# Linear attention on one core: the first head's k and v move from SyncE's DMA queue to ScalarE's

## The chip, the core and the metric

The kernel runs on one NeuronCore of one Trainium2 chip. A core has five engines with an instruction stream each: TensorE (PE, matrix products and transposes), VectorE (DVE), ScalarE (ACT), GpSimd (POOL) and SyncE (SP), which here only issues transfers. Transfers between HBM and the on-chip memory are carried out by 16 DMA engines, which are fed through queues; an engine that issues a transfer puts it into its own queue and goes on. The metric is the time of one execution on the device in microseconds; of several executions the median counts.

## The reference

For each of 32 heads (sequence length S = 2048, head width D = 128, bf16), linear attention with the feature map elu(x) + 1:

```python
phi_q = jnp.where(q > 0, q + 1, jnp.exp(q)) + 1e-6
phi_k = jnp.where(k > 0, k + 1, jnp.exp(k)) + 1e-6
kv = jnp.einsum("bhsd,bhse->bhde", phi_k, v)
z = jnp.einsum("bhsd->bhd", phi_k)
num = jnp.einsum("bhqd,bhde->bhqe", phi_q, kv)
den = jnp.einsum("bhqd,bhd->bhq", phi_q, z)[..., None] + 1e-6
return num / den
```

q, k and v have the shape (1, 32, 2048, 128), and so has the result. A head of one of these tensors is 512 KB.

## The kernel before

**Tiling.** A head is laid out as 128 partitions by 16 tiles of 128 elements, so that a load or store of a head moves 128 rows of 4096 bytes. The feature map is computed as min(exp(x), 1) + 1e-6 plus max(x, 0), and the two summands are kept apart: every product is two accumulating matmuls.

**Stages of a head h.** Each operation has a key, a letter code with the head and a part number:

- `ldk`, `ldq`, `ldv` (line 324) load k, q and v of the head into one of NI = 7 buffers each.
- For k: `ek` (line 336, ACT) takes the exponential, `em` (line 339, DVE) the minimum with 1 and the addition; `rkd` (line 342, DVE) and `rkp` (line 346, POOL) take max(k, 0) of one half each.
- `v1` (line 350, POOL) copies v beside a column of ones; `kv` (line 357, PE) makes the 128 x 129 matrix of kv and z, and `kvs` (line 362, ACT) copies it out.
- For q: `T` (line 368, PE) transposes q; `eq` (line 372, ACT), `emq` (line 374, DVE), `rqa` (line 378, ACT) and `rqb` (line 381, DVE) apply the feature map.
- `n` (lines 389, 394, 396, PE) makes numerator and denominator; `r` (line 403, DVE) is the reciprocal of the denominator and `f` (line 410, DVE) the product with it; `st` (line 418) stores the head.

In head 0 the operations on k, q and v are cut into two halves (parts .0 and .1), but its three loads are whole heads. The last head is cut more finely, its store into three parts.

**Order.** What each engine does in which order is written out by hand in the table `ORDER` (line 83). A small planner, `Program.resolve` (line 182), turns the dependencies between keys into semaphore waits; an engine works through its list strictly in order. PE begins with two groups of dummy matmuls on the identity matrix, `w2` and `w1` (4 each, line 315), then the two halves of `T0`, then `w0` (15 dummy matmuls), then `kv0`. ACT begins with

```python
eq0.0 eq0.1 ek0.0 ek0.1 rqa0 ek1.0 kvs0 eq1.0 rqa1 ek2.0 kvs1 ...
```

and SP, which issues every load and every store, begins with

```python
ldq0.0 ldk0.0 ldv0.0 ldk1.0 ldq1.0 ldv1.0 ldk2.0 ldq2.0 ldk3.0 ldv2.0 ldv3.0 ...
```

The first 21 loads have no buffer to wait for; a later one waits until its buffer has been read. Every load slot has a semaphore of its own; each of the 16 DMA engines raises it by one when its share has landed, and the reader waits for all 16. SP ends by waiting for all stores.

**Buffers that tie engines together.** `em`, `rk`, `v1`, `emq`, `rq` and `kvs` have two buffers each, so an engine may be at most two heads ahead of its reader. Through a `gate`, POOL starts `rkp` and `v1` of head h only after `f` or `r` of head h - 3.

Of the kernel before, what the change touches and what calls it, by code (L numbers as in the profile page):

```python
# [4 lines left out]
ACT = mybir.ActivationFunctionType  # L5
# [5 lines left out]
NI, NO, NE, NR, NV, NQ, NK = 7, 12, 2, 2, 2, 2, 2  # L11
WARM = (15, 4, 4)
HALVES = ((0, 8), (8, 16))
WHOLE = ((0, 16),)


def k_parts(h):
    return HALVES if h == 0 else WHOLE


def ld_parts(h):
    return WHOLE

# [4 lines left out]
def q_parts(h):  # L28
    return HALVES if h == 0 else ((0, 8), (8, 12), (12, 16)) if h == NH - 1 else WHOLE


def kv_parts(h):
    return HALVES

# [23 lines left out]
def st_parts(h):  # L58
    return ((0, 6), (6, 12), (12, 16)) if h == NH - 1 else WHOLE

# [10 lines left out]
def t_parts(h):  # L71
    return HALVES if h in (0, NH - 1) else WHOLE


def rqb_parts(h):
    if na(h) == 16:
        return ()
    if h == NH - 1:
# [34 lines left out]
        emq31.1 f29.1 r30.0 f30.0 r30.1 f30.1 r31.0 f31.0 r31.1 r31.2 f31.1 f31.2  # L113
    """,
    "ACT": """
        eq0.0 eq0.1 ek0.0 ek0.1 rqa0 ek1.0 kvs0 eq1.0 rqa1 ek2.0 kvs1 ek3.0 eq2.0 rqa2 kvs2 ek4.0 eq3.0 kvs3 rqa3
        ek5.0 eq4.0 kvs4 rqa4 ek6.0 eq5.0 kvs5 rqa5 ek7.0 eq6.0 kvs6 rqa6 ek8.0 eq7.0 kvs7 rqa7 ek9.0 eq8.0 kvs8
        rqa8 ek10.0 eq9.0 kvs9 rqa9 ek11.0 eq10.0 kvs10 rqa10 ek12.0 eq11.0 kvs11 rqa11 ek13.0 eq12.0 kvs12 rqa12
        ek14.0 eq13.0 kvs13 rqa13 ek15.0 eq14.0 kvs14 rqa14 ek16.0 eq15.0 kvs15 rqa15 ek17.0 eq16.0 kvs16 rqa16
# [10 lines left out]
        v128.0 rkp28.0 v129.0 rkp29.0 v130.0 rkp30.0 v131.0 rkp31.0  # L130
    """,
    "SP": """
        ldq0.0 ldk0.0 ldv0.0 ldk1.0 ldq1.0 ldv1.0 ldk2.0 ldq2.0 ldk3.0 ldv2.0 ldv3.0 ldk4.0 ldq3.0 ldv4.0 ldq4.0
        ldk5.0 ldv5.0 ldk6.0 ldq5.0 ldv6.0 ldv7.0 ldk7.0 ldq6.0 ldk8.0 ldq7.0 ldk9.0 ldk10.0 ldq8.0 ldv8.0 ldv9.0
        ldq9.0 st0.0 ldq10.0 ldq11.0 ldq12.0 st1.0 ldv10.0 ldk11.0 ldk12.0 ldv11.0 st2.0 ldv12.0 ldq13.0 ldk13.0
        ldv13.0 st3.0 ldk14.0 ldk15.0 st4.0 ldv14.0 ldv15.0 ldq14.0 ldk16.0 st5.0 ldk17.0 ldq15.0 ldv16.0 ldv17.0
# [19 lines left out]
class Program:  # L156
# [10 lines left out]
    def add(self, eng, key, fn, deps=(), dma=None, inc=True):  # L167
        assert key not in self.op, key
        self.op[key] = (eng, fn, tuple(deps), dma, inc)
# [71 lines left out]
def bass_standalone__linear_attn_elu__prompt_kernel(nc: bass.Bass, q: bass.AP, k: bass.AP, v: bass.AP, out: bass.AP):  # L241
# [9 lines left out]
    rows = lambda t, h: t[h].rearrange("(p j) d -> p j d", j=NT)  # L251

    with ExitStack() as es:
# [25 lines left out]
        add = pr.add  # L279
# [41 lines left out]
            warm(f"w{i}", n)  # L321

        def load(name, dst, src, h, i, t0, t1, last):
            add("SP", f"ld{name}{h}.{i}", lambda e: e.dma_start(dst[:, h % NI, t0:t1], rows(src, h)[:, t0:t1]),
                last, dma=f"{name}{h % NI}.{i}")

        def head(h):
            for i, (a, b) in enumerate(ld_parts(h)):
                load("k", k_sb, kf, h, i, a, b, freed(NI, h, ("ek", k_parts), ("rkd", rkd_parts), ("rkp", rkp_parts)))
            for i, (a, b) in enumerate(ld_parts(h)):  # L330
                load("q", q_sb, qf, h, i, a, b, freed(NI, h, ("T", t_parts)))
            for i, (a, b) in enumerate(ld_parts(h)):
                load("v", v_sb, vf, h, i, a, b, freed(NI, h, ("v1", v_parts)))
# [130 lines left out]
```

## Time and profile before

| what | value |
|---|---|
| median of 5 runs | 170.13 us (169.88 to 170.65) |
| the profiled execution, its own time | 170.95 us |
| its span, first to last instruction | 169.7 us |
| outside the span | 1.3 us |
| mean granted TensorE clock | 0.992 |
| busy PE, DVE, ACT, POOL | 159.6, 154.5, 153.9, 86.4 us |
| bytes read from and written to HBM | 50.33 MB, 16.78 MB |
| mean rate over the span | 396 GB/s |
| loads: from issue to landing, median | about 15.5 us |

The profiled execution is one execution, 0.8 us longer than the median of the runs. The profile lists the engines' busy time, the span in 40 slices, the DMA queues, the chain of work that ended last, and groups of instructions. "SPq" marks the issuing of a transfer by SP; the transfer itself lands later. The share of a DMA queue is the time of its packets as a share of 16 engines' span. In the table of stretches, the columns are the busy time of each engine with the number of instructions in brackets, the granted clock, the share of the DMA engines and what they moved; some of the DMA engines' packets overlap, so that a share can be over 1.

### The profile page before, as it was taken

Reading aid. Unit: us, or ns where it says so; the run is one execution under the profiler, and the core shown is the slowest. Engines: PE = TensorE matmul, PEld = TensorE weight load, DVE = VectorE, ACT = ScalarE, POOL = GpSimd, SP = SyncE. Lnnn points to the kernel's source line nnn. Section 1 sums busy time; section 2 is a strip of 40 time slices with the busy share of each in tenths; the row PEclk is TensorE's granted clock in tenths of the full one; section 3 lists DMA queues with packets and bytes.
Section 4 is the critical chain, followed back from the end, with each engine's and each line's share of the span. In section 5 each row is a group of like instructions: output and inputs, shape, how many; then the busy total and the mean of one; then the engine's idle time right before and its main releaser. Section 6 shows DMA issues by size and latency. Waiting matters only on the chain.

```text
span 169.7 us, 6310 instructions
## 1 busy us (share of the span) xinstructions
PE 159.6 (94%) x2775; PEld 154.3 (91%) x2775; DVE 154.5 (91%) x267; ACT 153.9 (91%) x133; POOL 86.4 (51%) x71
## 2 busy tenths in 40 slices
PE   6999789999999999999999999999999999999850
PEld 2679779999999999999999999999999999999840
DVE  0188999999999999999999999999999999999891
ACT  3699989999999999999999999999999999995800
POOL 1436926556665556555565556645556554535000
PEclk9999999999999999999999999999999999999996
DMA  5999999999999999999999999999999999999984
GB/s 210 328 417 415 408 409 408 406 412 404 417 414 408 415 414 413 418 412 422 409 416 415 413 418 414 411 420 414 417 413 416 416 415 420 414 414 417 389 336 168
DMA packets 18748, 67.53 MB, mean 398 GB/s; under 512 B 2080, under 2 KB 2464, under 8 KB 18720
## 3 DMA queue, kind: packets, MB, share of 16 engines
q1 hardware_dynamic: 18720, 67.12, 98.3%
q8 instruction: 22, 0.36, 0.8%
q14 instruction: 6, 0.05, 0.1%
HBM read 50.33 MB, written 16.78 MB: 396 GB/s over the span
## 4 chain that ended last, share of the span: by engine, by line
PE 88%; DVE 8%; issue 1%; POOL 0%; POOLq 0%
PE la L357 33%; PE la L394 18%; PE la L368 17%; PE la L396 16%; DVE la L410 4%; PE la L315 4%; DVE la L342 1%; DVE la L339 1%; PE la L389 1%; DVE la L381 1%; DVE la L403 1%; DVE la L374 0%; POOL la L301 0%; POOL la L300 0%; POOLq L301 0%
## 5 line engine op out<-in xcount | busy, mean ns | idle before, releaser
L410 DVE TENSOR_TENSOR la<-la 128x1536 bf16<-128x1536 f32 (+2 forms) x65 | 77.5, 1193 | 0.2
L396 PE MATMUL la<-la 128*128 128x129 bf16 x512 | 68.0, 220 | 0.0
L394 PE MATMUL la<-la 128*128 128x129 bf16 x512 | 68.0, 219 | 0.0
L372 ACT ACTIVATE la<-la 128x2048 bf16<-128x2048 bf16 (+2 forms) x35 | 60.3, 1731 | 5.7 <-PE la L368 3.8
L357 PE MATMUL la<-la 128*128 128x129 bf16 x1024 | 64.0, 219 | 0.6 <-DVE la L339 0.6
L350 POOL COPY la<-la 128x1024 int32<-128x1024 int32 (+1 forms) x33 | 41.3, 1252 | 40.0 <-DVE la L403 27.7
L336 ACT ACTIVATE la<-la 128x2048 bf16<-128x2048 bf16 (+1 forms) x33 | 61.3, 1860 | 0.0
L357 PEld LDWEIGHTS la<-la 128*128 128x128 bf16 x1024 | 60.0, 97 | 1.2 <-DVE la L339 0.8
L346 POOL TENSOR_SCALAR la<-la 128x1024 bf16<-128x1024 bf16 x32 | 44.6, 1395 | 27.8 <-DVE la L410 23.6
L396 PEld LDWEIGHTS la<-la 128*128 128x128 bf16 x512 | 49.5, 97 | 0.0
L394 PEld LDWEIGHTS la<-la 128*128 128x128 bf16 x512 | 47.1, 97 | 0.0
L368 PE MATMUL la<-la 128*128 128x128 bf16 x512 | 34.6, 222 | 0.4 <-DVE la L381 0.4
L389 PE MATMUL la<-la 128*128 128x3 bf16 (+1 forms) x192 | 32.3, 168 | 2.1 <-DVE la L410 1.6
L378 ACT ACTIVATE la<-la 128x1024 bf16<-128x1024 bf16 (+1 forms) x32 | 33.5, 1046 | 0.0
L368 PEld LDWEIGHTS la<-la 128*128 128x128 bf16 x512 | 30.0, 99 | 1.3 <-DVE la L381 0.5
L339 DVE TENSOR_SCALAR la<-la 128x2048 bf16<-128x2048 bf16 (+1 forms) x33 | 23.6, 715 | 3.3 <-ACT la L336 3.1
L389 PEld LDWEIGHTS la<-la 128*128 128x128 bf16 x192 | 18.7, 97 | 2.9 <-DVE la L410 2.0
L342 DVE TENSOR_SCALAR la<-la 128x1024 bf16<-128x1024 bf16 x32 | 17.1, 534 | 4.6 <-DMA la<-in_k_dram 4.6
L374 DVE TENSOR_SCALAR la<-la 128x2048 bf16<-128x2048 bf16 (+2 forms) x35 | 20.9, 599 | 0.3 <-ACT la L372 0.3
L381 DVE TENSOR_SCALAR la<-la 128x1024 bf16<-128x1024 bf16 x31 | 20.8, 672 | 0.0
L403 DVE RECIPROCAL la<-la 128x12 f32<-128x12 f32 (+2 forms) x65 | 12.7, 196 | 2.1 <-PE la L396 1.0
L362 ACT ACTIVATE la<-la 128x129 bf16<-128x129 f32 x32 | 9.0, 282 | 0.4 <-PE la L357 0.4
(14 smaller groups left out, 11.8 us busy)
## 6 DMA issues: line engine op xcount, KB each, us to landing
la<-in_q_dram SPq DMA_DIRECT2D x32, 512.0 KB, 15.4
la<-in_k_dram SPq DMA_DIRECT2D x32, 512.0 KB, 15.5
la<-in_v_dram SPq DMA_DIRECT2D x32, 512.0 KB, 15.5
out_dram<-la SPq DMA_DIRECT2D x31, 512.0 KB, 15.7
out_dram<-la SPq DMA_DIRECT2D x2, 192.0 KB, 2.7
out_dram<-la SPq DMA_DIRECT2D x1, 128.0 KB, 3.6
```

Source lines behind the costliest of these rows:

```text
L336: add("ACT", f"ek{h}.{i}", lambda e, a=a, b=b: e.activation(em_sb[:, h % NE, a:b], k_sb[:, h % NI, a:b], ACT.Exp), over("ldk", h, ld_parts ...
L339: add("DVE", f"em{h}.{i}", lambda e, a=a, b=b: e.tensor_scalar(em_sb[:, h % NE, a:b], em_sb[:, h % NE, a:b], 1.0, EPS, op0=ALU.min, op1=AL ...
L346: add("POOL", f"rkp{h}.{i}", lambda e, a=a, b=b: e.tensor_scalar(rk_sb[:, h % NR, a:b], k_sb[:, h % NI, a:b], BIG, 0.0, op0=ALU.min, op1=A ...
L350: add("POOL", f"v1{h}.{i}", lambda e, a=a, b=b: e.tensor_copy(v1_sb[:, h % NV, a:b, 0:D].bitcast(i32), v_sb[:, h % NI, a:b].bitcast(i32)), ...
L357: ins = e.matmul(kv_ps, lhsT=src[:, j], rhs=v1_sb[:, h % NV, j, 0:NC], start=(j + part == 0), stop=(j == NT - 1 and part == 1))
L368: ins = e.transpose(xT[:, j], q_sb[:, h % NI, j], ident[:])
L372: add("ACT", f"eq{h}.{i}", lambda e, a=a, b=b: e.activation(emq_sb[:, h % NQ, a:b], xT[:, a:b], ACT.Exp), over("T", h, t_parts, a, b) + fr ...
L378: add("ACT", f"rqa{h}", lambda e: e.activation(rq_sb[:, h % NQ, 0:n], xT[:, 0:n], ACT.Relu), over("T", h, t_parts, 0, n) + freed(NQ, h, (" ...
L389: e.matmul(_ap(o_ps[:, :], o + D, [[NC, m]]), lhsT=ones[:], rhs=epsr[:, 0:m], start=True, stop=False, skip_group_check=True)
L394: e.matmul(to, lhsT=emq_sb[:, h % NQ, t], rhs=kvs_sb[:, h % NK], start=False, stop=False, skip_group_check=True)
L396: ins = e.matmul(to, lhsT=rq_sb[:, h % NQ, t], rhs=kvs_sb[:, h % NK], start=False, stop=True, skip_group_check=True)
L410: return e.tensor_tensor(out=_ap(o_sb[:, :, :, :], first(o_sb[:, h % NO, t0, 0:1]) - first(o_sb[:, :, :, :]), [[m * D, nb], [D, m], [1, D] ...
```

## The change

The two loads `ldk0.0` and `ldv0.0` are taken out of SP's list and put at the head of ACT's. The loader asks a new tuple, `BY_ACT`, which engine issues a load. SP's list then begins with q of head 0 and k of head 1. No wait, buffer, size or other order is touched.

```diff
@@
 HALVES = ((0, 8), (8, 16))
+BY_ACT = ('ldk0.0', 'ldv0.0')
 WHOLE = ((0, 16),)
@@ ORDER, "ACT"
-        eq0.0 eq0.1 ek0.0 ek0.1 rqa0 ek1.0 kvs0 eq1.0 rqa1 ek2.0 kvs1 ek3.0 eq2.0 rqa2 kvs2 ek4.0 eq3.0 kvs3 rqa3
+        ldk0.0 ldv0.0 eq0.0 eq0.1 ek0.0 ek0.1 rqa0 ek1.0 kvs0 eq1.0 rqa1 ek2.0 kvs1 ek3.0 eq2.0 rqa2 kvs2 ek4.0 eq3.0 kvs3 rqa3
@@ ORDER, "SP"
-        ldq0.0 ldk0.0 ldv0.0 ldk1.0 ldq1.0 ldv1.0 ldk2.0 ldq2.0 ldk3.0 ldv2.0 ldv3.0 ldk4.0 ldq3.0 ldv4.0 ldq4.0
+        ldq0.0 ldk1.0 ldq1.0 ldv1.0 ldk2.0 ldq2.0 ldk3.0 ldv2.0 ldv3.0 ldk4.0 ldq3.0 ldv4.0 ldq4.0
@@ load
         def load(name, dst, src, h, i, t0, t1, last):
-            add("SP", f"ld{name}{h}.{i}", lambda e: e.dma_start(dst[:, h % NI, t0:t1], rows(src, h)[:, t0:t1]),
+            add("ACT" if f"ld{name}{h}.{i}" in BY_ACT else "SP", f"ld{name}{h}.{i}", lambda e: e.dma_start(dst[:, h % NI, t0:t1], rows(src, h)[:, t0:t1]),
                 last, dma=f"{name}{h % NI}.{i}")
```

## The prediction

> **What bounds the kernel now.** I read the page first: the busy line, the slices and the queue.
>
> ```profile
> span 169.7 us, 6310 instructions
> PE 159.6 (94%) x2775; PEld 154.3 (91%) x2775; DVE 154.5 (91%) x267; ACT 153.9 (91%) x133; POOL 86.4 (51%) x71
> DMA  5999999999999999999999999999999999999984
> q1 hardware_dynamic: 18720, 67.12, 98.3%
> ```
>
> Two things are full at once: PE with DVE, and the one DMA queue, whose packets fill 98.3% of 16 engines' span. The end tells which of them closes the run, so next come the end's timeline and the stretches near it.
>
> ```profile
> 164.28 2.02 SPq L418 DMA_DIRECT2D out_dram<-la  x3
> 164.41 1.53 DVE L410 TENSOR_TENSOR la<-la 128x768 bf16<-128x768 f32 x2
> ...
> 157.00:159.00 2.00, 2.00 (x40) 2.00 (x38) 1.62 (x4) 2.00 (x5) 0.00 (x0) 1.00 1.05 424
> 161.00:163.00 2.00, 0.88 (x17) 0.89 (x18) 1.84 (x3) 0.00 (x0) 0.00 (x0) 1.00 0.84 340
> 167.00:168.00 1.00, 0.00 (x0) 0.00 (x0) 0.00 (x0) 0.00 (x0) 0.00 (x0) 0.50 0.52 188
> 168.00:169.00 1.00, 0.00 (x0) 0.00 (x0) 0.00 (x0) 0.00 (x0) 0.00 (x0) 0.50 0.07 25
> ```
>
> DVE is done at 165.94, and the last store is issued then. The DMA engines are full until 159, then some run dry (0.84), and after 168 hardly one is left (0.07). The completion events of the last store's semaphore, one for each DMA engine and part, say it finely: all but four come by 168.27, and the rest at 168.33 (the store before), 168.83, 169.30 and 169.61. Those four look like one engine that is 1.34 us behind the others; its steps before that, 163.13, 164.53, 165.84, 167.11, 168.33, are about 1.28 us, one whole transfer each. So in this execution the last 1.34 us belong to one late DMA engine that never ran dry, and compute has that much cover.
>
> Then the start, where the change acts: issues, first users, and the time to landing of the first four transfers.
>
> ```profile
> 0.73 1.28 ACT L372 ACT_TABLE_LOAD   x1 [0.73 <-PEq L449]
> 0.74 0.38 SPq L324 DMA_DIRECT2D la<-in_q_dram  x1
> 1.17 0.42 SPq L324 DMA_DIRECT2D la<-in_k_dram  x1
> 4.70 1.89 PE L368 MATMUL la<-la 128*128 128x128 bf16 x16
> 5.80 1.94 ACT L372 ACTIVATE la<-la 128x1024 bf16<-128x1024 bf16 x2 [3.79 <-PE la L368]
> 8.05 1.17 POOL L350 COPY la<-la 128x512 int32<-128x512 int32 x2 [1.26 <-DMA la<-in_v_dram]
> 9.65 2.00 PE L357 MATMUL la<-la 128*128 128x129 bf16 x32
> ...
> la<-in_q_dram SPq DMA_DIRECT2D x1, 512.0 KB, 3.3
> la<-in_k_dram SPq DMA_DIRECT2D x1, 512.0 KB, 4.3
> la<-in_v_dram SPq DMA_DIRECT2D x1, 512.0 KB, 6.4
> la<-in_k_dram SPq DMA_DIRECT2D x1, 512.0 KB, 7.2
> ```
>
> Issue plus landing: q0 at 4.06, k0 at 5.45, v0 at 8.00, k1 at 9.32 (semaphore events); q1, v1, k2 and q2 follow at 10.60, 11.88, 13.16 and 14.44, 1.28 us apart. An issue takes SP only 0.38 to 0.46 us, so transfers, not issues, set these times. From `T0` on ACT is gapless to `kvs0` at 12.22, which releases `n0` at 12.66; the reciprocal at 14.31 waits for that, and from there DVE has hardly a gap.
>
> One thing is odd, in the stretches of the start:
>
> ```profile
> 4.00:4.50 0.50, 0.50 (x3) 0.21 (x2) 0.00 (x0) 0.00 (x0) 0.00 (x0) 1.00 0.84 344
> 4.50:5.00 0.50, 0.50 (x5) 0.30 (x3) 0.00 (x0) 0.00 (x0) 0.00 (x0) 1.00 0.66 221
> ```
>
> Some DMA engines stand idle although several transfers have been issued. Nine engines land v0 by 6.90 and seven at 7.40 to 8.00; those seven stay behind in k1, q1 and v1. This stall of up to 0.85 us carries into everything later.
>
> **The change, part by part.** (1) SP loses two issues, 0.42 each; its next ones come 2 x 0.47 = 0.94 us sooner (k1 at 1.17, not 2.11). Worth nothing while transfers queue: from the eighth issue on the rows grow from 0.44 to 1.0 us and landing takes 15 us. (2) ACT gains two issues, 2 x 0.43 = 0.86 by SP's rows. If the table load stays with the first activation, it slips from 0.73 to about 1.6 and ends near 2.9; `eq0.0` starts at 5.80, so 2.9 us of waiting cover it. No new wait is added; behind the issues on ACT stand only the table load and `eq0.0`. (3) Bytes and packets are the same, so each DMA engine's work is the same. From the fifth transfer on, the order of arrival is the same too.
>
> (4) What does change is who shares with whom: q0 no longer goes alone. Both queues issue at about 0.74. The trace of before has one queue for data and can't show how an engine divides itself between two. Bounds from its rows: q0 keeps its 4.06 (it goes first), or lands with k0 at 5.45, 1.39 later. Even sharing, row by row, is my value: q0 needs 16 row times instead of 8, less a little for a head start, and lands at about 5.3. v0 then shares with k1 and lands with it at 9.3 instead of 8.00.
>
> [...]
>
> (5) What late q0 does: PE is busy with dummies until 4.91 anyway, and `T0`'s first weights were loaded 0.24 after q0 landed. With 5.3 they come at 5.55, the first transpose at about 5.6 rather than 4.70 to 4.91: +0.7 to +0.9, say +0.75. ACT is gapless behind it, so `kvs0` and `n0` move by 0.75 as well. (6) Late v0: `v10.0` ends at 9.3 + 0.6 = 9.9, which alone would hold `kv0` by 0.25 (9.65 before); but `em0.0` now ends at 9.50 + 0.75 = 10.25, so v0's delay hides behind q0's. If q0 isn't late, 0.25 is the whole delay. (7) The delay runs on through DVE, where line 342 takes 1.26 at 17.36 against 0.43 at 5.47 while POOL works; I pass it on undiminished. Compute ends at 165.94 + 0.75 = 166.7.
>
> **The sum**, against the profiled execution: fifteen DMA engines end at 168.27 + 0.75 = 169.0; the late one still ends at 169.61, as its queue is never empty: the last store needs to be there only shortly before. So +0.0 on 170.95. The median of the runs, 170.13, is 0.82 lower than that execution, and I don't see where. If all of it comes off the late engine, that engine ends at 168.79 and compute shows by 169.0 - 168.79 = 0.2. I take +0.15: 170.3, bounds -0.2 (nothing late, a bit of the stall filled) to +0.5.
>
> **Rivals.** *Slower, uncovered:* in the runs without a profile the late engine isn't late and compute ends last; then q0's delay passes whole, 0.5 to 0.95: 170.13 + 0.8 = 170.9. For it: those 0.82 us; PE's chain of waits holds 88% of the span. Against it: 98.3%, and the single straggler. It decides once the straggler's lead over compute is under 0.3.
>
> *Slower, cold PE:* between the dummies and `T0` PE now idles some 0.7 us. The first 8 dummies of 480 columns take 3.38 us, 0.42 each, the 15 of `w0` 3.22, 0.21 each: the clock doubles in between, about when `T0` ends. If the gap puts this off, `w0` costs up to 15 x 0.21 = 3.1 us more; less the cover of 1.34, 0 to 1.8, middle 1.0: 171.1. Against it: the gap is short beside 3.4 us of work before it. [...]
>
> *Faster, the stall goes:* with a second ring the seven engines have other descriptors at 4.3 to 5.2. The late engine ends up to 0.85 sooner, at 168.76, and compute bounds at 168.3 to 169.0: -0.6 to -0.85, so 169.4. For it: idle engines with work issued. Against it: nothing shows that the ring was the cause.
>
> *It doesn't do as said:* ACT's table load goes first (1.28 us), k0 is issued at 2.0, q0 goes alone and k0 and v0 come late by some 2.5 us (to 8.0 and 10.6). `kv0` starts at about 11.2, +1.6, of which the 1.34 cover nearly all: 170.4.
>
> **Chances.** Forecast 0.36 (same 0.31, slower 0.03, faster 0.02); uncovered 0.28 (slower 0.23, same 0.05); cold PE 0.10, slower; stall gone 0.20 (faster 0.19, same 0.01); table load first, or whole transfers in turn with q0 first, 0.06 (same 0.05, faster 0.01). Together faster 0.22, same 0.42, slower 0.36, with 0.3% (0.51 us) as about what a measurement of this kernel can tell from no change. The range: 169.5 to 171.1 leaves out half of the cold case and half of the stall case; the forecast's own is 169.9 to 170.65.
>
> **What would show it.** Right: q0 lands near 5.3 and v0 near 9.3, `T0` starts near 5.6, DVE ends near 166.7, and the last landing hardly moves. Wrong: q0 still at 4.06 (whole transfers in turn); `w0` at 0.42 each (cold); no dip below 0.9 of DMA share at 4.5 to 5.0 (stall gone); a landing that follows DVE's end by the same 3.67 us as before (uncovered).

## The result and the profile after

The changed kernel takes 171.01 us (median of 30 runs, 170.74 to 172.18), the kernel before, run beside it, 170.30 us (54 runs, 169.55 to 171.0). The ratio is 1.0044 (95% interval 1.0033 to 1.0055): 0.7 us slower. The recorded time, 170.3, missed by that 0.7: it allowed 0.15 for the change. The range, 169.5 to 171.1, holds the result because it was drawn wide enough for the rivals; the forecast's own, 169.9 to 170.65, does not.

The profiled execution of the changed kernel took 172.18 us; it is the slowest of the 30, so it shows more than the typical loss. Its page (in the changed kernel's profiles every line from 14 on has a number higher by one):

```profile
span 170.9 us, 6308 instructions
PE 160.9 (94%) x2775; PEld 154.5 (90%) x2775; DVE 154.7 (91%) x267; ACT 154.0 (90%) x133; POOL 87.3 (51%) x71
DMA  5999999999999999999999999999999999999756
q1 hardware_dynamic: 18432, 66.07, 95.8%
q10 hardware_dynamic: 288, 1.05, 1.6%
```

The new queue carries 288 packets, two heads of 128 rows each and their semaphore writes. The DMA engines now run dry earlier at the end (7, 5, 6 tenths in the last three slices; 9, 8, 4 before): work, not transfers, closes this execution. The timeline of its start, and the transfers' time to landing:

```profile
0.73 0.41 ACTq L325 DMA_DIRECT2D la<-in_k_dram  x1
0.74 0.37 SPq L325 DMA_DIRECT2D la<-in_q_dram  x1
1.16 0.42 SPq L325 DMA_DIRECT2D la<-in_k_dram  x1
1.17 0.46 ACTq L325 DMA_DIRECT2D la<-in_v_dram  x1
1.66 1.28 ACT L373 ACT_TABLE_LOAD   x1 [1.66 <-PEq L450]
5.63 1.89 PE L369 MATMUL la<-la 128*128 128x128 bf16 x16 [0.72 <-DMA la<-in_q_dram]
6.71 1.94 ACT L373 ACTIVATE la<-la 128x1024 bf16<-128x1024 bf16 x2 [3.76 <-PE la L369]
7.32 4.61 PE L316 MATMUL la<-la 128*128 128x480 bf16 x15
8.60 1.16 POOL L351 COPY la<-la 128x512 int32<-128x512 int32 x2 [1.49 <-DMA la<-in_v_dram]
11.76 2.00 PE L358 MATMUL la<-la 128*128 128x129 bf16 x32
...
la<-in_q_dram SPq DMA_DIRECT2D x1, 512.0 KB, 4.8
la<-in_k_dram ACTq DMA_DIRECT2D x1, 512.0 KB, 5.0
la<-in_k_dram SPq DMA_DIRECT2D x1, 512.0 KB, 7.1
la<-in_v_dram ACTq DMA_DIRECT2D x1, 512.0 KB, 7.4
```

By the semaphore events q0 lands at 5.59 (before 4.06), k0 at 5.76 (5.45), k1 at 8.22 (9.32), v0 at 8.54 (8.00). PE stands idle for 0.72 us and waits for q0; `T0` starts at 5.63, `eq0.0` at 6.71 instead of 5.80. Behind it the 15 dummy matmuls of `w0` take 4.61 us; the trace's granted clock rises at 10.15 us, not at 6.44, so half of them ran at the slow clock (they start 0.40 us apart up to 10.12, then 0.20), and `kv0` waits for them until 11.76.

The stretches of the start that had the stall before, and the end:

```profile
4.00:4.50 0.50, 0.50 (x3) 0.05 (x1) 0.00 (x0) 0.00 (x0) 0.00 (x0) 1.00 1.02 377
4.50:5.00 0.50, 0.41 (x2) 0.00 (x0) 0.00 (x0) 0.00 (x0) 0.00 (x0) 1.00 1.08 434
...
163.00:165.00 2.00, 0.52 (x11) 0.34 (x8) 1.97 (x3) 0.32 (x1) 0.00 (x0) 1.00 0.77 313
165.00:167.00 2.00, 1.92 (x37) 1.74 (x34) 1.77 (x5) 0.00 (x0) 0.00 (x0) 1.00 0.37 139
```

No DMA engine stalls at 4.5 to 5.0 any more (1.08 against 0.66), and everything from k1 to v3 lands 0.9 to 1.2 us sooner. It buys nothing at the end: at 165 to 167 the DMA share is 0.37, and the transfers wait for DVE, which ends at 168.59 (165.94 before).

One loss sits far from the change. Between `kv27` and `kv28` PE's starts are 5.50 us apart in this profile, where all steps around it, and this one before, are 4.72. The timeline of DVE and POOL there, first before, then after:

```profile
136.61 0.22 DVE L403 RECIPROCAL la<-la 128x12 f32<-128x12 f32 x1
136.75 0.36 DVE L342 TENSOR_SCALAR la<-la 128x1024 bf16<-128x1024 bf16 x1
137.02 0.68 DVE L374 TENSOR_SCALAR la<-la 128x2048 bf16<-128x2048 bf16 x1
137.11 1.48 POOL L350 COPY la<-la 128x1024 int32<-128x1024 int32 x1 [0.95 <-DVE la L342]
```

```profile
138.47 0.22 DVE L404 RECIPROCAL la<-la 128x12 f32<-128x12 f32 x1
138.61 0.36 DVE L343 TENSOR_SCALAR la<-la 128x1024 bf16<-128x1024 bf16 x1
138.75 1.11 POOL L351 COPY la<-la 128x1024 int32<-128x1024 int32 x1 [0.77 <-DVE la L404]
138.89 1.52 DVE L375 TENSOR_SCALAR la<-la 128x2048 bf16<-128x2048 bf16 x1
```

`emq26.0` takes 0.68 us when it starts 0.09 before POOL's copy of v (which then takes 1.48 instead of 1.11), and 1.52 when the copy starts 0.14 before it. Before, `r25.0` ended at 136.83, but head 28's v landed only at 136.99, and the copy started at 137.11, 0.09 behind `emq26.0` (the profile names as its releaser `rkd28.0`, which ends at the same moment). After, v had landed at 137.12 and the copy started as soon as `r25.0` released it, at 138.75, while DVE still had `rkd28.0` ahead of `emq26.0`. In these rows the one that starts second takes longer, by 0.84 us (`emq26.0`) or 0.37 (the copy); by what mechanism isn't shown.

### The profile page after: what moved, and what is told of

Same layout as the page of the kernel before. It is cut to its first block, busy times and chain, and to the rows that moved or that the text cites. A ratio compares the mean times of both kernels' runs of the same rounds, so it can differ in the third digit from the quotient of the medians.

```text
span 170.9 us, 6308 instructions
## 1 busy us (share of the span) xinstructions
PE 160.9 (94%) x2775; PEld 154.5 (90%) x2775; DVE 154.7 (91%) x267; ACT 154.0 (90%) x133; POOL 87.3 (51%) x71
## 4 chain that ended last, share of the span: by engine, by line
ACT 67%; PE 19%; DVE 9%; DMA 3%; issue 0%; DVEq 0%
ACT la L373 26%; ACT la L337 25%; ACT la L379 12%; PE la L358 7%; DVE la L411 5%; PE la L369 4%; ACT la L363 4%; PE la L395 3%; DMA la<-in_q_dram 3%; PE la L397 3%; PE la L316 3%; DVE la L375 1%; DVE la L343 1%; DVE la L340 1%; DVE la L382 1%; DVE la L404 1%
## 5 line engine op out<-in xcount | busy, mean ns | idle before, releaser
L347 POOL TENSOR_SCALAR la<-la 128x1024 bf16<-128x1024 bf16 x32 | 45.1, 1410 | 33.5 <-DVE la L411 26.4
L340 DVE TENSOR_SCALAR la<-la 128x2048 bf16<-128x2048 bf16 (+1 forms) x33 | 22.7, 687 | 3.9 <-ACT la L337 3.9
L375 DVE TENSOR_SCALAR la<-la 128x2048 bf16<-128x2048 bf16 (+2 forms) x35 | 21.9, 629 | 0.3 <-ACT la L373 0.3
```

Source lines behind the costliest of these rows:

```text
L340: add("DVE", f"em{h}.{i}", lambda e, a=a, b=b: e.tensor_scalar(em_sb[:, h % NE, a:b], em_sb[:, h % NE, a:b], 1.0, EPS, op0=ALU.min, op1=AL ...
L347: add("POOL", f"rkp{h}.{i}", lambda e, a=a, b=b: e.tensor_scalar(rk_sb[:, h % NR, a:b], k_sb[:, h % NI, a:b], BIG, 0.0, op0=ALU.min, op1=A ...
```

## The experiments

**Theory 1:** q0, which alone starts PE's and ACT's work, shares the DMA engines with k0 and lands 1.5 us late; all of compute is late, and nothing covers it. **Rivals:** the second queue costs something of its own; the gap before `T0` puts off the faster clock; the loss comes by way of collisions between POOL and DVE, not by the delay itself. Each time stands beside the median of the kernel before in the same set of runs, and the ratios are to that; between sets this median lies at 170.15 to 170.49.

**Head start for q0** (two queues):
```diff
@@ load
-                last, dma=f"{name}{h % NI}.{i}")
+                last + (["ident"] if f"ld{name}{h}.{i}" in BY_ACT else []), dma=f"{name}{h % NI}.{i}")
```


> ACT's two loads wait for the identity matrix (ready at about 1.47 us), so they are issued at about 1.5 and 2.0 us instead of 0.73 and 1.17, and q of head 0 has a head start of some 0.8 us on its DMA queue. Theory 1 (q0 late because it shares the DMA engines): q0 lands near 4.7 instead of 5.6, the transposes follow the dummies without a gap, ACT starts at 5.8 to 5.9, and the time falls back to the kernel before or a little under it, 169.9 to 170.4. Theory 2 (a second queue costs something by itself): no change from the changed kernel, 171.0.

171.54 us against 170.49, ratio 1.0092 (1.0056 to 1.0128). Neither number came. q0 landed at 4.03, alone; but SP had put k1 in next, and k1 landed (5.28) before k0 (7.40) and v0 (9.96). `T0` started at 4.70 again and `kv0` only at 10.95. There it had waited 1.60 us for the copy of v0. The twelve runs spread from 171.0 to 173.55. The test moved the delay from q to k and v and does not decide; it shows that a late v0 costs as well.

**k0 before q0, one queue:**
```diff
@@ ORDER, "SP" (the line's beginning)
-        ldq0.0 ldk0.0 ldv0.0 ldk1.0
+        ldk0.0 ldq0.0 ldv0.0 ldk1.0
```


> The kernel before, one queue, with k of head 0 ahead of q of head 0 on SP. Theory 1 (a late q0 is the whole cause): q0 lands near 5.5 without any second queue, the gap before the transposes is about 0.7 us, and the time is that of the changed kernel, 170.8 to 171.2. Theory 2 (the second queue costs): the time stays at 170.1 to 170.4.

170.87 against 170.49, 1.0034 (1.0011 to 1.0056). Without a second queue q0 lands at 5.34, `T0` starts at 5.39, and most of the loss is there (the intervals overlap). A cost of the second queue as such is not needed.

**Two more dummies in `w1`, and a shorter `w0`** (two queues):
```diff
-WARM = (15, 4, 4)
+WARM = (15, 6, 4)   # the first kernel
+WARM = (7, 4, 4)    # the second
```


> The changed kernel with two more dummy matmuls (6 instead of 4 in w1), so that PE doesn't idle from 4.9 to 5.6 us. Theory A (the idle gap puts off the faster PE clock, and the dummies of w0, still slow, hold back kv0): w0 takes about 3.2 us as before, kv0 starts at 10.2 to 10.5 instead of 11.8, and the time falls by 0.3 to 1.0 us to about 170.2 to 170.7. Theory B (the gap doesn't matter; the clock's rise falls where it falls, and late q0 costs by ACT's gapless chain alone): within 0.2 of the changed kernel, 170.9 to 171.2.

> The changed kernel with 7 instead of 15 dummy matmuls in w0. Theory A (the dummies of w0 hold back kv0 while the clock is slow): kv0 starts when em0.0 and the copy of v are done, at about 10.2, and the time falls to 170.2 to 170.7. Theory B (ACT's chain behind the late q0 is what costs, 0.9 us): kv0 starts at about 10.2 too, but the sum stays near that of typical runs of the changed kernel, 170.8 to 171.1; it may be slower if the clock rises later for want of work.

With the gap (nearly) filled: 171.06, 1.0038 (1.0018 to 1.0057), as the changed kernel, but no run above 171.49. Its profile has `w0` at full clock:

```profile
5.62 1.07 PE L369 MATMUL la<-la 128*128 128x128 bf16 x16 [0.24 <-DMA la<-in_q_dram]
6.53 3.20 PE L316 MATMUL la<-la 128*128 128x480 bf16 x15
10.15 2.00 PE L358 MATMUL la<-la 128*128 128x129 bf16 x32 [0.42 <-DVE la L306]
```

`kv0` starts 1.6 us sooner than in the changed kernel's profile, yet the median doesn't move: the slow `w0` explains that one execution, not the median. With the short `w0` the median is 171.99 (1.0085, 1.0054 to 1.0115), slower, though its profiled execution (171.24) has the same start, `kv0` at 10.10. Why the others take longer was not found.

**k0 alone on ACT,** v0 second on SP, and the same with the gap filled:
```diff
-BY_ACT = ('ldk0.0', 'ldv0.0')
+BY_ACT = ('ldk0.0',)
@@ ORDER, "ACT" and "SP" (the lines' beginnings)
-        ldk0.0 ldv0.0 eq0.0
+        ldk0.0 eq0.0
-        ldq0.0 ldk1.0 ldq1.0
+        ldq0.0 ldv0.0 ldk1.0 ldq1.0
+WARM = (15, 6, 4)   # the second kernel only
```


> Of the changed kernel, k of head 0 alone goes through ACT; v of head 0 is second on SP. Theory 1 (sharing makes q0 late, whoever the partner): q0 lands near 5.6, the transposes start near 5.6, time as the changed kernel, 170.9 to 171.1. Theory 2 (v0 behind k1 matters too): v0 lands earlier than 8.5 and the time falls by 0.3 or more.

> The kernel with k of head 0 alone on ACT (172.0) and two more dummy matmuls in w1, so that PE has no gap before the transposes. Theory 1 (the gap puts off the faster clock in most of its runs; the dummies of w0 then hold back kv0): w0 takes 3.1 to 3.3 us, kv0 starts at 10.0 to 10.3 instead of 11.9, and the time falls by about 1 us to 170.8 to 171.2. Theory 2 (something else in that order costs): it stays at 171.8 to 172.2.

172.04 (1.0110, 1.0082 to 1.0138) and 171.73 (1.0074, 1.0057 to 1.0091). In the first q0 lands at 5.54 and `T0` starts at 5.59, so k0 as q0's partner is enough to make it late. The time is 1 us worse than forecast. In its profile the clock rises at 10.43, `w0` takes 4.8 us, and the last landing, 171.37, comes 0.7 us after the one before it. With the gap filled `kv0` starts at 9.67, sooner even than Theory 1 said, but the time falls only by 0.3 (by the ratios 0.6): DVE ends at 167.62, and the last landing comes at 170.40, where all others are done by 169.55. What makes it late stays open.

**The kernel before, again,** and both kernels with one step of DVE moved, so that `emq26.0` follows `r25.0` at once:
```diff
@@ ORDER, "DVE" (within a line)
-f24.1 r25.0 rkd28.0 emq26.0 f25.0
+f24.1 rkd28.0 r25.0 emq26.0 f25.0
```


> The kernel before, once more, for a second profile and as a comparison of a kernel with itself: ratio 1.000. Its runs of so far lie in two groups, about 169.6 to 170.2 and 170.4 to 171.0. Theory 1 (one collision on VectorE in head 26, 0.8 us, that takes place in some runs): a profile from the upper group shows an emq (line 374) of about 1.5 us near 137 and 5.5 us instead of 4.7 between kv27 and kv28, one from the lower group doesn't. Theory 2 (a late DMA engine at the end makes the upper group): the profile shows stores landing on one engine over 1 us after the others and no long emq.

> The kernel before with rkd28.0 ahead of r25.0 in VectorE's list, so that emq26.0 follows r25.0 at once and GpSimd's copy of v, which r25.0 releases, can't slip in before it. Theory 1 (collision): no emq of 1.5 us, the upper group of runs is gone, median 169.6 to 169.9. Theory 2: the median stays at 170.3.

> The changed kernel with the same step moved. Theory 1 (the change costs 0.9 us at the start, and the collision adds 0.8 us in nearly every run): no emq of 1.5 us, 170.2 to 170.5, that is 0.8 less than the changed kernel and 0.6 to 0.9 more than the kernel before with the same step moved. Theory 2 (the start's delay is all there is, and covered or not by DMA): no change from 171.0.

The kernel before with itself: 170.31 against 170.47, 0.9990 (0.9972 to 1.0008). Its profile (170.79) has the 5.50 us step at `kv27`, and no late DMA engine: its last ten landings lie within 0.13 us. With the step moved it takes 169.80, 0.9971 (0.9952 to 0.9991); the changed kernel takes 170.25, 0.9996 (0.9981 to 1.0011), 0.76 less than its 171.01 in another set. The 5.50 step is gone from both profiles. So the collision in head 26 is worth 0.5 to 0.8 us; it is in every profile in which the step was not moved, but for the first of the kernel before.

Between the two kernels with the step moved 0.45 us remains. There are collisions at the start too. The second profile of the kernel before shows them:

```profile
10.84 1.04 POOL L350 COPY la<-la 128x1024 int32<-128x1024 int32 x1 [2.68 <-DMA la<-in_v_dram]
10.91 1.25 DVE L374 TENSOR_SCALAR la<-la 128x1024 bf16<-128x1024 bf16 x1
12.10 1.24 DVE L342 TENSOR_SCALAR la<-la 128x1024 bf16<-128x1024 bf16 x1
13.54 0.17 DVE L308 MEMSET la<- 128x128 bf16 x1
13.77 0.18 PE L389 MATMUL la<-la 128*128 128x3 bf16 x1 [1.62 <-DVE la L308]
```

v1 had landed at 10.79, POOL copied it 0.07 us ahead of `emq0.1`, DVE lost some 0.8 twice (in `emq0.1`, 1.25 against 0.42 in the rows further down, and in `rkd1.0`, 1.24 against 0.42 in the one-queue profile with both moves), and the memset of `ones`, last in that queue, held back `n0.0` for 1.62 us. In the kernel before with `rkd28.0` moved, `emq0.1` came first and took 0.42, `rkd1.0` behind it still took 1.25, and `n0.0` waited 0.80:

```profile
10.73 0.42 DVE L374 TENSOR_SCALAR la<-la 128x1024 bf16<-128x1024 bf16 x1
10.82 1.22 POOL L350 COPY la<-la 128x1024 int32<-128x1024 int32 x1 [2.65 <-DMA la<-in_v_dram]
```

**Memsets first.** DVE idles until k lands, so the memsets can be made there. With one queue, with two, and with two and the gap filled:
```diff
@@ ORDER, "DVE" (within two lines)
-v1ones0 rkd0.0 em0.0 eps0 em0.1 v1ones1 emq0.0 rqb0.0 emq0.1 eps1 rkd1.0 eps2 ones em1.0 r0.0
+v1ones0 v1ones1 eps0 eps1 eps2 ones rkd0.0 em0.0 em0.1 emq0.0 rqb0.0 emq0.1 rkd1.0 em1.0 r0.0
-f24.1 r25.0 rkd28.0 emq26.0 f25.0
+f24.1 rkd28.0 r25.0 emq26.0 f25.0
+WARM = (15, 6, 4)   # the third kernel only
```


> One queue as in the kernel before, rkd28.0 ahead of r25.0, and the small memsets (v1ones1, eps0 to eps2, ones) at the head of VectorE's list, where it idles until k lands at 5.4. In three profiles n0.0 waited for the memset ones, for 0.8 to 1.6 us, behind VectorE operations that GpSimd had held up. Theory 1 (these collisions set the start): n0.0 starts at about 12.4 and the time is 169.1 to 169.6, under the 169.8 with rkd28.0 alone. Theory 2 (em1.0 and the reciprocal come when they come): no change from 169.8.

> Two queues as in the changed kernel with both of these moves. Theory 1 (late q0 costs the same wherever the collisions are): 0.5 to 0.9 us above the same kernel with one queue, 169.8 to 170.3. Theory 2 (the change costs only by way of the collisions): within 0.2 of the one-queue kernel.

> The two-queue kernel with both moves (169.7) and two more dummy matmuls in w1, so that PE has no gap before the transposes. Theory 1 (the gap now and then puts off the faster clock, as in one of the twelve runs, 171.1): the median stays at 169.5 to 169.8 and no run is above 170.3. Theory 2 (the gap plays no part): the same median, with a run above 170.8 now and then.

One queue: 169.94, 0.9971 (0.9955 to 0.9987), no gain over `rkd28.0` alone. Two queues: 169.72, 0.9971 (0.9950 to 0.9993). Theory 1 expected the second 0.5 to 0.9 above the first; **they are the same.** q0 still lands at 5.60 and `T0` still starts at 5.65. With the gap filled as well: 169.77, 0.9967 (0.9947 to 0.9987), all twelve runs between 169.55 and 169.88, while the kernel with the gap had one at 171.12 (in the profile with two more dummies the clock rises at 4.27, so they run fast and 0.6 us of the gap stays). This one is 0.33% faster than the kernel before.

Equal medians don't mean that a late q0 costs nothing by itself. In the profile with one queue the reciprocal `r0.0` starts at 13.88, 1.0 us before the two-queue kernel's 14.89, and `kv2` at 19.59 against 20.63; but `kv5` starts at 33.83 against 33.95. Two steps lose the lead: from `kv2` to `kv3` it takes 4.12 where the other takes 3.87, and from `kv3` to `kv4` 5.39 where the other takes 4.72. In the first one `rkd3.0` comes behind a copy and takes 1.25 (0.41 in the two-queue profile). In the second one head 4's v had landed at 22.76 when:

```profile
18.97 1.45 POOL L350 COPY la<-la 128x1024 int32<-128x1024 int32 x1
19.45 1.25 DVE L342 TENSOR_SCALAR la<-la 128x1024 bf16<-128x1024 bf16 x1
...
22.90 1.04 POOL L350 COPY la<-la 128x1024 int32<-128x1024 int32 x1 [2.48 <-DMA la<-in_v_dram]
23.05 1.44 DVE L374 TENSOR_SCALAR la<-la 128x2048 bf16<-128x2048 bf16 x1
```

A copy that waited for its load came just ahead of `emq3.0`. So in this profile the lead was lost to collisions of its own; in how many of the twelve runs it is so, one profile can't say.

The profiles side by side (us; the last column is the execution's own time less DVE's end):

| kernel | `T0` | `r0.0` | `kv5` | long `emq26.0` | DVE ends | own time | after DVE |
|---|---|---|---|---|---|---|---|
| before | 4.70 | 14.31 | 33.69 | no | 165.94 | 170.95 | 5.01 |
| before again | 4.71 | 15.44 | 34.47 | yes | 167.50 | 170.79 | 3.29 |
| before, `rkd28.0` moved | 4.71 | 14.43 | 33.54 | no | 165.80 | 169.50 | 3.70 |
| before, both moves | 4.70 | 13.88 | 33.83 | no | 166.24 | 169.92 | 3.68 |
| k0 first, one queue | 5.39 | 15.30 | 34.42 | yes | 167.46 | 170.78 | 3.32 |
| after | 5.63 | 16.15 | 35.55 | yes | 168.59 | 172.18 | 3.59 |
| after, head start for q0 | 4.70 | 15.36 | 34.75 | yes | 167.79 | 171.07 | 3.28 |
| after, gap filled | 5.62 | 15.55 | 34.58 | yes | 167.61 | 171.13 | 3.52 |
| after, short `w0` | 5.62 | 15.51 | 34.53 | yes | 167.68 | 171.24 | 3.56 |
| k0 alone on ACT | 5.59 | 16.27 | 35.66 | yes | 168.69 | 172.72 | 4.03 |
| k0 alone on ACT, gap filled | 5.53 | 15.48 | 34.51 | yes | 167.62 | 171.75 | 4.13 |
| after, `rkd28.0` moved | 5.54 | 15.56 | 34.59 | no | 166.85 | 170.49 | 3.64 |
| after, both moves | 5.65 | 14.89 | 33.95 | no | 166.22 | 169.81 | 3.59 |
| after, both moves, gap filled | 5.66 | 14.93 | 33.98 | no | 166.23 | 169.69 | 3.46 |

From `kv5` on hardly anything but the collision in head 26 tells the profiles apart: DVE ends 132.25 to 132.41 us after `kv5` starts, or 133.03 to 133.15 where `emq26.0` is long.

## Why the prediction was right and wrong

**Right in the main, step by step.** The issues cost nothing, on either engine: ACT's took 0.41 and 0.46, its table load slipped to 1.66 and ended at 2.94 (forecast 1.6 and 2.9), the first activation came 3.8 us later. q0 does share, and never kept its 4.06; but at 5.59 it came 0.29 later than forecast, and past the bound of 5.45. That `T0` still started at 5.63 as forecast (5.6) is luck: it followed the landing by 0.04 us, not by the 0.3 that was counted. v0 lay hidden behind q0, at 8.54 (9.3). And the order of landing from q1 on is the same.

**The step that failed is the cover**, "the late one still ends at 169.61 ... So +0.0". It was read from one execution. The straggling DMA engine, 1.34 us behind, is not in the second profile of the kernel before, whose last ten landings lie within 0.13 us, nor in that with `rkd28.0` moved, whose last one comes 0.18 behind the one before it. There the own time is 3.3 and 3.7 us after DVE's end, as in nearly every profile of the table, and DVE's delay is the run's. The profiled 170.95 lay near the top of the runs because of that engine; these two executions end with work. The rival that named this, "Slower, uncovered", gave 170.9 and had 0.28; the 0.82 us between profile and median, counted there in its favour, was the hint to follow. Its upper value for q0's delay, 0.95, is shown by no run; `eq0.0` came 0.91 later (6.71 against 5.80).

**"I pass it on undiminished" holds from `kv5` on, and left out the collisions.** What is late at `kv5` is late at DVE's end, by the table to within 0.2 us, and a collision in head 26 adds 0.8. Up to `kv5`, and in head 26, the landing times decide which of DVE's operations come just behind POOL's copies, and the kernel before loses there too: in its second profile DVE ends at 167.50, as late as in the changed kernel with its gap filled (167.61). That fits its runs' spread of 1.4 us, against 0.5 for those of the changed kernel, but for two. The prediction had such a collision in hand, line 342 at 1.26 us instead of 0.43, and priced it at nothing.

The medians differ by 0.7 us with the orders as they were, by 0.45 with the step in head 26 moved, and by nothing clear of the noise with the memsets moved as well (169.72 against 169.94). So how much a late q0 costs depends on which collisions each kernel meets. How the 0.7 splits between the delay itself and the collisions isn't shown: the ratios have intervals of about 0.2% to either side, and there is one profile for each order.

**Cold PE** happened in the profiled execution (4.61 us for `w0`), with `kv0` 1.6 us later than with the gap filled. It doesn't set the median, as filling the gap left it at 171.06. **The stall going** (with a second queue, the prediction's ring) happened as well, and was priced wrongly: transfers 1 us sooner shortened nothing here, where work ended last (DMA share 0.37 at 165 to 167), and a v that has landed when DVE is at work can even hurt, as in head 28, where its copy started 0.14 ahead of `emq26.0`, which took 1.52 instead of 0.68. **The table load first** did not happen.

## What to carry to other kernels

Where operations of two engines lengthen each other, as those of VectorE and GpSimd do here (`emq26.0` took 0.68 or 1.52 us), a delay of a few tenths does more than pass on: it also decides who comes first at each meeting, and a meeting lost cost up to 0.8 us here. So a kernel that starts sooner can lose its lead again, as the one with one queue and both moves did (1.0 us ahead of two queues at `r0.0`, 0.12 at `kv5`). Look for the pairs that start close together (0.07 to 0.15 us in the rows above), above all where one side is released by a load, and order the lists so that the engine on the critical path issues straight after the event that releases the other (in head 26 that was worth 0.5 to 0.8 us).

A second queue for the first loads gave the transfer that starts everything a partner to share with (q0 landed at 5.59, not 4.06); keep that transfer alone in front without putting the next ones off, as the single queue did here, and don't call a delay covered by a straggler that one profile shows.

## What the runs showed of the hardware

- In the changed kernel the DMA engines served both queues side by side: from 2.5 to 5.5 us 152 packets of SP's queue started and 159 of ACT's. No engine's share of q0 landed before 5.04 us, and k0's shares landed between 5.25 and 5.76, where q0's alone had landed between 3.62 and 4.06. Neither of the two went through whole ahead of the other.
- With the loads held until 1.50 us the sharing was not even: SP's second transfer landed at 5.28, ACT's first, issued 0.34 us after it, at 7.40.
- The stall of some DMA engines near 4.5 us (v0 at 7.8 to 8.0 rather than 6.9) is in 3 of 5 profiles with one queue and in none of those in which both k0 and v0 are issued by ACT at the start. Its cause was not tried.
- The granted clock rose between 4.3 and 6.5 us in all profiles without a gap before `T0`, with two more dummies, or with a gap of 0.5 us, and at 10.15 and 10.43 in two with a gap of 0.7 us. In three others with a gap of 0.6 to 0.8 us it rose at 4.81, 5.01 and 5.95, the first two before the gap or at its very start (4.91). So the length of the gap alone doesn't tell when it rises, and what does isn't shown.
